# V weights early, K and Q weights as halves, remainder rows in one transfer, and a new written-out order

## The chip, the cores and the metric

One core of one Trainium2 chip. The metric is device time in microseconds (us) of one execution; the median of three runs of the kernel before is 170.06 us. PE is TensorE, DVE VectorE, ACT ScalarE, POOL GpSimd, and SP the engine whose queue issues nearly all transfers.

## The reference

A block with adaptive layer norm over x of 2048 x 448 (bfloat16): a sliding-window attention (16 heads of 28, each position sees 8 positions 2 apart) and a mixer MLP (448 to 1792 to 448).

```
mod = (silu(c) @ w_mod).reshape(...)           # sa, ca, ga, sb, cb, gb, 448 each
h = layernorm(x) * (1 + ca) + sa
q, k, v = split(h @ wqkv)                      # wqkv: 448 x 1344
o = softmax(q . k at 8 offsets, step 2) . v
x = x + ga * (o @ wo)
h = layernorm(x) * (1 + cb) + sb
x = x + gb * (gelu(layernorm(h) @ w1 + b1) @ w2 + b2)
```

## The kernel before

The 2048 rows are 8 tiles p of 2 x 128 rows. Per tile a layer norm (stats, rstd, normalize) gives zy, which is transposed and scaled by the modulation into hT (features on the partitions). Tiles 0 and 1 are transposed on PE (L534); tiles 2 to 7 by DMA transposes that SP issues (L526). Then K, Q and V projections, attention in 9 batches, output projection, second norms, and the MLP, whose two products (L547 with w1, L882 with w2) fill the second half of the run.

Inputs have 448 = 3 x 128 + 64 features. Each weight is therefore loaded as three full blocks of 128 rows and a **remainder** of 64 rows, which is stored twice, on partitions 0 to 63 and 64 to 127, so that two half-height matmuls can use both halves of the array. In the kernel before each copy of a remainder is a transfer of its own: two for the modulation (wm_r, L348), two for K and Q together (wqr_st, L328), two for V (Wv, L334). The three full blocks of K and Q come as one transfer per block, Q and K columns together (wqk_st, L324). "Spread" copies bring Q and K weights from wqk_st and wqr_st into Wqk and Wqr with 32 columns per head; they run on DVE, ACT or POOL (L438 to L449). For tiles 0 and 1 the projections of Q (half 0) and K (half 1) use Wqk and Wqr (`front_qk`, L561, L547, L553); tiles 2 to 7 use wqk_st and wqr_st directly (`natural_qk`).

Nothing is scheduled by the compiler. Every piece of work is recorded as a numbered task, and the string ORDER gives the sequence in which the tasks are written out: each engine executes its own tasks in just that sequence, and waits at the head of its queue for what its next task reads. `55+12@55` means that 12 dummy matmuls on a zero tile (`filler`, L381) are written ahead of task 55; a letter chooses the engine. SLOTS assigns each buffer its place in a pool. Transfers on SP go out in that order too, and eight completion counters take turns: a transfer is issued only after the one eight places ahead of it (ACT's two loads of c are counted in) has landed.

The loads stand in this order before the change: x tile 0, modulation weights (wm_st, then wm_r twice), x tile 1, K and Q weights block by block with their remainders between, x tiles 2 and 3, x tiles 6 and 7, V weights, x tiles 4 and 5. V of batches 0 and 1 is computed after K and Q of tiles 0 and 1.

Of the kernel before, what the change touches and what calls it, by code (L numbers as in the profile page):

```python
# [55 lines left out]
200 141 199 128 269 125 271 236 270 130 207 40 209 33 201 241 210 38 237 208 272 238 273 37 185 242 152 202 35 154 151
153:A 8 278 187 239 203 159 211 204 188 205:D 212 206 155 279 213 186 243 240 214:A 160 156 192 215 307 157 189 275
161 274 158 280 171 308 281 282 193 162 172 244 245 284 195 283 163 217 173 285 246 276:D 219 39 218 167 216 277 247
447 164 196 248 225 286 168 224 165 169:D 174 312 42 309 313 228 166 310 314 220 170 226 311 290 221 289 229 222 288
315 194 287 230 558 232 197 317 176 560 233 318 175 316 177 223 249 319 234 49 227 320 250 231 251 559 321 235 345 253  # L60
# [13 lines left out]
662 653 627 665 655 657 652 663 659 674 660 666 667 669 661 675 668 676 678 677 679 686 672 673 670 687 681 671 690
680 691 688 689 694 693 701 683 692 682 684 695 685 702 697 703 704 709 698 696 710 699 705 711 700 706 712 707 708
# [77 lines left out]
def kernel(  # L153
# [166 lines left out]
    def rows128(src):  # L320
        return src.rearrange("(k p) n -> p k n", p=128)

    def load_qk(kt):
        load(lambda: nc.sync.dma_start(out=wqk_st.t[:, kt, :], in_=A_wqkv[kt * 128:kt * 128 + 128, 0:2 * D + HP - DH]), 0.62, [f"wqk{kt}"],  # L324
             bufs=[wqk_st])

    def load_rest(a):
        load(lambda a=a: nc.sync.dma_start(out=wqr_st.t[KS * a:KS * a + KS, :], in_=A_wqkv[(KT - 1) * 128:D, 0:2 * D + HP - DH]),  # L328
             0.5, [f"wr{a}"], bufs=[wqr_st])
# [17 lines left out]
    for v in range(2):  # L347
        load(lambda v=v: nc.sync.dma_start(out=wm_r.t[KS * v:KS * v + KS, :], in_=w_mod[(KT - 1) * 128:D, v * D:v * D + D]),  # L348
             0.25, [f"wmr{v}"], bufs=[wm_r])
    for kt in range(KT - 1):  # L350
        load_qk(kt)
# [38 lines left out]
    add("PE", 0.45, c_cols, mode="32x128", reads=["c", "c1", "one1", "warm_w"], bufs=[psc], fills=[psc], name="c_cols")  # L390
    add("ACT", 0.12, lambda: nc.scalar.activation(out=e_c[:], in_=psc.t[:, 0, 0:128 * KT:128], func=ACT.Exp, scale=-1.0), bufs=[psc],
# [39 lines left out]
    def spread(half):  # L431
        def heads(ap, h):
            return bass.AP(ap.tensor, ap.offset, [*ap.ap[:-1], [DH, h], [1, HP]])

        for ks in [[k] for k in range(KT - 1)]:
            k0, n = ks[0], len(ks)
            dst, src = (lambda k0=k0, n=n: Wqk[:, k0:k0 + n, half]), (lambda k0=k0, n=n: heads(wqk_st.t[:, k0:k0 + n, half * D:half * D + D], H))
            add("DVE", 0.06 + 0.18 * n, lambda dst=dst, src=src: nc.vector.tensor_copy(out=dst(), in_=src()), reads=[f"wqk{k}" for k in ks],  # L438
                bufs=[wqk_st], writes=[f"W{half}{k}" for k in ks], port=True, name="spread",
                alt={"ACT": (0.13 + 0.43 * n, lambda dst=dst, src=src: nc.scalar.copy(out=dst(), in_=src())),  # L440
                     "POOL": (0.1 + 0.5 * n, lambda dst=dst, src=src: nc.gpsimd.tensor_copy(out=dst(), in_=src()))})

        for a in range(2):
            rows, c0 = slice(KS * a, KS * a + KS), half * D + a * D // 2
            src = lambda rows=rows, c0=c0: heads(wqr_st.t[rows, c0:c0 + D // 2], H // 2)
            add("DVE", 0.22, lambda rows=rows, src=src: nc.vector.tensor_copy(out=Wqr[rows, half], in_=src()), reads=[f"wr{a}"],
                bufs=[wqr_st], writes=[f"Wr{half}{a}"], port=True, name="spread r",
                alt={"ACT": (0.33, lambda rows=rows, src=src: nc.scalar.copy(out=Wqr[rows, half], in_=src())),
                     "POOL": (0.4, lambda rows=rows, src=src: nc.gpsimd.tensor_copy(out=Wqr[rows, half], in_=src()))})  # L449
# [59 lines left out]
    def front_ln(u, on_act, dma=False):  # L509
# [5 lines left out]
        for q, p in enumerate(u):  # L515
# [3 lines left out]
            rstd(0, 2 * p, 2, on_act)  # L519
# [59 lines left out]
    def front_qk(u):  # L579
        last_qk.clear()  # L580
        n, c0 = 128 * len(u), LEAD + 128 * u[0]
        for half in range(2):
# [30 lines left out]
    def natural_qk(p):  # L613
        c0 = LEAD + 128 * p
        for half in (1, 0):
# [6 lines left out]
            summed([item(s) for s in range(NS)], 0.1895, [f"wqk{k}" for k in range(KT - 1)] + ["wr0", "wr1"] + [f"h{kt}_{p}" for kt in range(KT)],  # L622
# [54 lines left out]
    def attention(i, tbl, prev_w1):  # L677
# [5 lines left out]
        if i not in DIRECT:  # L683
            hw = sb("hw", [128, KT, NS, 2, WK], BF16, "hw")

            def windows(copy):
# [8 lines left out]
                     lambda kt, rows: Wv[rows, kt, :]) for s in range(NS)], 0.1895, ["wv", "wvr0", "wvr1"],  # L695
                   [pv, vb, hw], [pv], f"v{i}")
        else:
# [19 lines left out]
            add("PE", 7 * 0.1895 + 0.1, None, reads=["pads", "wv", "wvr0", "wvr1"] + [f"h{kt}_{p}" for kt in range(KT) for p in ps_], bufs=[pv, vb],  # L717
# [244 lines left out]
```

## Time and profile before

| What | Value |
|---|---|
| median of 3 runs | 170.06 us (169.41 to 172.02) |
| the profiled execution | 170.37 us, of which 168.6 us lie between first and last instruction (the span) |
| PE busy | 160.9 us of the span |
| DVE, ACT, POOL busy | 113.2, 101.3, 42.0 us |
| moved by DMA | 18.78 MB, mean 111 GB/s |
| TensorE clock granted | 1.000 |

Times in the rows are us from the start of the span. A row of the timeline gives start, length, engine, source line, operation and tiles, a count, and in brackets how long the engine was idle before it and what ended that. The rows for stretches give, for each engine, busy us and (count).

### The profile page before, as it was taken

Reading aid. Unit: us, or ns where it says so; the run is one execution under the profiler, and the core shown is the slowest. Engines: PE = TensorE matmul, PEld = TensorE weight load, DVE = VectorE, ACT = ScalarE, POOL = GpSimd, SP = SyncE. Lnnn points to the kernel's source line nnn. Section 1 sums busy time; section 2 is a strip of 40 time slices with the busy share of each in tenths; the row PEclk is TensorE's granted clock in tenths of the full one; section 3 lists DMA queues with packets and bytes.
Section 4 is the critical chain, followed back from the end, with each engine's and each line's share of the span. In section 5 each row is a group of like instructions: output and inputs, shape, how many; then the busy total and the mean of one; then the engine's idle time right before and its main releaser. Section 6 shows DMA issues by size and latency. Waiting matters only on the chain.

```text
span 168.6 us, 4965 instructions
## 1 busy us (share of the span) xinstructions
PE 160.9 (95%) x2126; PEld 84.0 (50%) x2126; DVE 113.2 (67%) x277; ACT 101.3 (60%) x139; POOL 42.0 (25%) x69
## 2 busy tenths in 40 slices
PE   7999969987999999999999999999999999999992
PEld 4778535444554544435565443555544455344562
DVE  7869898758899969897837869465596940400112
ACT  3378888949379946869557167986318440099000
POOL 3235251002030400319300033850003156008100
PEclk9999999999999999999999999999999999999999
DMA  5999989699999799300150000028020006110002
GB/s 158 323 336 291 167 253 172 129 158 255 188 227 287 211 160 201 100 0 0 25 106 2 4 0 2 4 49 188 4 95 14 0 4 120 46 67 0 0 27 82
DMA packets 35573, 18.78 MB, mean 111 GB/s; under 512 B 28507, under 2 KB 34592, under 8 KB 35552
## 3 DMA queue, kind: packets, MB, share of 16 engines
q1 hardware_dynamic: 35548, 18.47, 47.6%
q8 instruction: 16, 0.26, 0.6%
q14 instruction: 5, 0.04, 0.1%
q10 hardware_dynamic: 4, 0.00, 0.0%
HBM read 9.81 MB, written 1.84 MB: 69 GB/s over the span
## 4 chain that ended last, share of the span: by engine, by line
PE 77%; DMA 13%; DVE 4%; issue 2%; POOL 2%; SPq 1%; ACT 1%; POOLq 0%; DVEq 0%
PE p L882 26%; PE p L547 22%; PE pw L802 7%; DMA zT<-zy 7%; PE pq L547 5%; PE p L553 4%; DMA x_all<-in_A_x_dram 4%; PE pv L547 3%; PE po L770 3%; DMA wm_st<-in_w_mod_dram 3%; PE lt L737 2%; DVE hT L501 2%; PE pv L705 2%; PE pd L759 1%; DVE stt L455 1%
## 5 line engine op out<-in xcount | busy, mean ns | idle before, releaser
L863 ACT ACTIVATE hm<-p,b_col 128x512 bf16<-128x512 f32 x56 | 33.6, 695 | 30.6 <-PE p L553 26.1
L882 PE MATMUL p<-w_s,hm 128*128 128x448 bf16 (+1 forms) x238 | 44.5, 342 | 0.0
L547 PE MATMUL p<-yT,w_s 128*128 128x512 bf16 x168 | 38.1, 380 | 0.0
L468 POOL TENSOR_TENSOR rs_all<-mvs,neg_half 128x2 f32<-128x2 f32 x23 | 16.4, 719 | 75.1 <-DVE mvs L457 75.1
L882 PEld LDWEIGHTS <-hm 128*128 128x128 bf16 x238 | 22.6, 98 | 18.9 <-issue 0.6
L547 PEld LDWEIGHTS <-w_s 128*128 128x128 bf16 x168 | 15.8, 98 | 21.0 <-issue 3.2
L888 DVE TENSOR_TENSOR x_all<-p,x1p 128x896 bf16<-128x896 f32 (+2 forms) x10 | 8.8, 899 | 23.7 <-PE p L882 23.7
L744 ACT ACTIVATE et<-lt 128x928 bf16<-128x928 f32 x18 | 16.1, 940 | 6.7 <-PE lt L737 6.6
L455 DVE BATCH_NORM_STATS2 stt<-x_all 128x6 f32<-128x448 bf16 x32 | 18.6, 610 | 1.6 <-DMA x_all<-in_A_x_dram 1.4
L547 PE MATMUL pq<-wqk_st,hT 128*128 128x448 bf16 x72 | 15.0, 353 | 1.8 <-DVE hT L501 1.5
L840 POOL TENSOR_TENSOR x1p<-x_all,gbb_bc 128x448 f32<-128x448 bf16 x16 | 16.5, 1060 | 0.0
L787 DVE TENSOR_TENSOR qT<-po,den 128x912 bf16<-128x912 f32 x9 | 10.0, 1106 | 7.1 <-ACT den L781 6.7
L802 PE MATMUL pw<-wo_s,qT 128*128 128x448 bf16 x64 | 13.1, 353 | 0.0
L750 DVE TENSOR_TENSOR et<-et,mask 128x928 bf16<-128x928 bf16 x18 | 11.0, 640 | 2.2 <-ACT et L744 2.1
L627 ACT CAST zy<-pq 128x896 bf16<-128x896 f32 x11 | 9.7, 911 | 2.7 <-issue 2.0
L809 DVE TENSOR_TENSOR x_all<-pw,x_all 128x896 bf16<-128x896 f32 x8 | 8.7, 1088 | 3.9 <-PE pw L802 3.9
L779 ACT ACTIVATE den<-pd 128x928 f32<-128x928 f32 x9 | 8.5, 952 | 4.7 <-PE pd L759 4.7
L818 DVE TENSOR_TENSOR h<-h,mod_bc 128x896 bf16<-128x896 bf16 x16 | 10.4, 655 | 0.2
L547 PEld LDWEIGHTS <-hT 128*128 128x128 bf16 x72 | 6.5, 98 | 8.1 <-DVE hT L501 2.0
L455 DVE BATCH_NORM_STATS2 stt<-h 128x6 f32<-128x448 bf16 x16 | 9.5, 611 | 0.1
L781 ACT ACTIVATE den<-den,den_bias 128x928 f32<-128x928 f32 x9 | 9.4, 1068 | 0.2
L802 PEld LDWEIGHTS <-qT 128*128 128x128 bf16 x64 | 6.0, 98 | 6.0 <-issue 0.4
(114 smaller groups left out, 177.3 us busy)
## 6 DMA issues: line engine op xcount, KB each, us to landing
w_s<-in_B_w_dram SPq DMA_DIRECT2D x7, 224.0 KB, 3.3
out_dram<-x_all SPq DMA_DIRECT2D x7, 224.0 KB, 2.0
x_all<-in_A_x_dram SPq DMA_DIRECT2D x3, 448.0 KB, 6.5
wmod<-in_w_mod_dram SPq DMA_DIRECT2D x3, 448.0 KB
w_s<-in_B_w_dram SPq DMA_DIRECT2D x3, 448.0 KB, 4.8
wqk_st<-in_A_wqkv_dram SPq DMA_DIRECT2D x3, 225.0 KB, 4.3
wm_st<-in_w_mod_dram SPq DMA_DIRECT2D x1, 672.0 KB, 4.6
x_all<-in_A_x_dram SPq DMA_DIRECT2D x2, 224.0 KB
```

The source lines that it names most:

```text
L455: add("DVE", 0.53, lambda: nc.vector.bn_stats(out=stt[:, w, b, 0:6], in_=src()), reads=reads, bufs=bufs, after=early if w == b == 0 else ( ...
L468: ways = {"POOL": (0.55 + 0.17 * n, lambda: nc.gpsimd.tensor_tensor(out=r, in0=v, in1=neg_half[:, 0:n], op=ALU.pow))}
L547: nc.tensor.matmul(out(), lhsT=lhs(kt, slice(0, 128)), rhs=rhs(kt, slice(0, 128)), start=first and kt == 0, stop=not first and kt == KT - 2)
L627: add("ACT", 0.80, lambda to=to, src=src: nc.scalar.copy(out=to(), in_=src()), bufs=[pq, st], reads=["zpad"], writes=[(st, 0)], name="evac ...
L744: exps.append(add("ACT", 0.83, lambda half=half, lt=lt: nc.scalar.activation(out=et.t[:, 2 * half:2 * half + 2].rearrange("p r m c -> p r ...
L750: nc.vector.tensor_tensor(out=ev, in0=ev, in1=mask[:], op=ALU.mult)
L787: nc.vector.tensor_tensor(out=qT[:, :, LEAD + q00:LEAD + q00 + 2 * WQ], in0=po.t[:, :, 0:NS * 4 * WQ].rearrange("p j (m c) -> p m j c", c=WQ),
L802: nc.tensor.matmul(pw.t[:, s, 0:D], lhsT=qT[:, KT * s + ft, LEAD + 128 * p:LEAD + 128 * p + 128], rhs=wo_s[:, ft, :], start=(ft == 0), sto ...
L818: add("DVE", 0.55, lambda vec=vec, op=op: nc.vector.tensor_tensor(out=h2.t[:], in0=h2.t[:], in1=vec.unsqueeze(1).to_broadcast([128, NS, D] ...
L840: add("POOL", 1.0, lambda n=n: nc.gpsimd.tensor_tensor(out=x1p.t[:, n, :], in0=xn(p, n), in1=gbb2_bc[:], op=ALU.add), reads=[f"x{p}", "gbb ...
L863: gelus.append(add("ACT", 0.585, lambda f=f, a=a, p1=p1s[g]: nc.scalar.activation(out=hm.t[:, f].rearrange("p n c -> p (n c)"), in_=p1.t[: ...
L882: nc.tensor.matmul(p2.t[:, n, 0:c1 - c0], lhsT=hm.t[:, f, n, q * 128:(q + 1) * 128], rhs=w2_s[:, f, c0:c1], start=(f == parts[0][0]), stop ...
```

## The change

1. Each remainder becomes one transfer (`twin`): the source is described as 2 x 64 rows, where the step of the outermost dimension is 448 columns for the modulation's and 0 for the others (the same 64 rows twice); the destination is 128 partitions. There are four: wm_r, Wv's, and one each for the K and the Q remainder.
2. The full blocks of K and Q come as two transfers, first all of K, later all of Q, instead of three transfers of both.
3. The V weights are loaded directly behind the modulation's; x tile 1, K and Q follow.
4. V of batch 0 stands in ORDER ahead of all K and Q projections. The layer norm of tile 0 takes its rstd one half at a time.
5. Dummy matmuls can be placed on carrier tasks of their own; 10 stand ahead of V of batch 0, 9 at the very end, 25 earlier (35 in all before the change, 44 after it). ORDER and SLOTS are new.

```diff
-    def load_qk(kt):
-        load(... out=wqk_st.t[:, kt, :], in_=A_wqkv[kt * 128:kt * 128 + 128, 0:2 * D + HP - DH]), 0.62, [f"wqk{kt}"], ...
-    def load_rest(a):
-        load(... out=wqr_st.t[KS * a:KS * a + KS, :], in_=A_wqkv[(KT - 1) * 128:D, 0:2 * D + HP - DH]), 0.5, [f"wr{a}"], ...
+    def load_half(half):
+        c0, c1 = half * D, half * D + D + half * (HP - DH)
+        load(... out=wqk_st.t[:, :, c0:c1], in_=rows128(A_wqkv[0:(KT - 1) * 128, c0:c1])), 1.15, [f"wqk{half}"], ...
+        load(... out=wqr_st.t[:, c0:c1], in_=twin(A_wqkv, c0, c1 - c0)), 0.4, [f"wr{half}"], ...
+
+    def twin(w, c0, n, step=0):
+        ld = w.ap[0][0]
+        return bass.AP(w.tensor, w.offset + (KT - 1) * 128 * ld + c0, [[step, 2], [ld, KS], [1, n]])
...
-        for a in range(2):
-            load(... out=Wv[KS * a:KS * a + KS, KT - 1, :], in_=A_wqkv[(KT - 1) * 128:D, 2 * D:3 * D]), 0.2, [f"wvr{a}"])
+        load(... out=Wv[:, KT - 1, :], in_=twin(A_wqkv, 2 * D, D)), 0.4, ["wvr"])
...
-    for v in range(2):
-        load(... out=wm_r.t[KS * v:KS * v + KS, :], in_=w_mod[(KT - 1) * 128:D, v * D:v * D + D]), 0.25, [f"wmr{v}"], ...
+    load(... out=wm_r.t[:], in_=twin(w_mod, 0, D, D)), 0.4, ["wmr"], bufs=[wm_r])
...
-            rstd(0, 2 * p, 2, on_act)
+            for b, m in ((2 * p, 1), (2 * p + 1, 1)) if p == 0 else ((2 * p, 2),):
+                rstd(0, b, m, on_act)
...
-3 14 17 0 1 15 5 9 10 18 11 16 13 19 20 2 6 24 21 73 55+12@55 26 12 71 25 56 72 74 57 75 22 58 77 23 59 62 60 27 61 76
+3 15 17 0 1 14 11 6 10 18 60+1@60 5 16 13 19 7 20 9 24 8 21 78 52+9@52 22 2 12 61 79 76 27 62 77 23 63 64 4 65 26 81
```

What stands in a row on the engines, at three places (names are tiles, destination before source; a count follows where rows are alike):

SP's queue at the program's start, before:

```order
L338 DMA x_all<-in_A_x_dram 128x896
L345 DMA wm_st<-in_w_mod_dram 128x3x896
L348 DMA wm_r<-in_w_mod_dram 64x448 x2
L338 DMA x_all<-in_A_x_dram 128x896
L324 DMA wqk_st<-in_A_wqkv_dram 128x900
L328 DMA wqr_st<-in_A_wqkv_dram 64x900 x2
L324 DMA wqk_st<-in_A_wqkv_dram 128x900 x2
L338 DMA x_all<-in_A_x_dram 128x2x896 x2
L332 DMA Wv<-in_A_wqkv_dram 128x3x448
```

SP's queue at the program's start, after:

```order
L338 DMA x_all<-in_A_x_dram 128x896
L345 DMA wm_st<-in_w_mod_dram 128x3x896
L347 DMA wm_r<-in_w_mod_dram 128x1x448
L334 DMA Wv<-in_A_wqkv_dram 128x3x448
L338 DMA x_all<-in_A_x_dram 128x896
L335 DMA Wv<-in_A_wqkv_dram 128x1x448
L326 DMA wqk_st<-in_A_wqkv_dram 128x3x452
L338 DMA x_all<-in_A_x_dram 128x2x896
L327 DMA wqr_st<-in_A_wqkv_dram 128x1x452
L327 DMA wqr_st<-in_A_wqkv_dram 128x1x448
L326 DMA wqk_st<-in_A_wqkv_dram 128x3x448
L338 DMA x_all<-in_A_x_dram 128x2x896 x2
```

V's weights moved from the thirteenth transfer to the fourth. The last Q weights went out as the tenth transfer; now they are the eleventh, behind all four remainders, whose rows read 128x1. L326 and L327 are `load_half`, L334 and L335 `load_wv`.

DVE's queue around the second norm of x tile 1 (zy) and the spreads (Wqk), before:

```order
L438 COPY Wqk<-wqk_st 128x512
L477 TENSOR_SCALAR zy_96<-x_all,mvs,rs_all 128x448 x2
L438 COPY Wqk<-wqk_st 128x512
L490 COPY zy_96<-zy_96 128x2x64
L438 COPY Wqk<-wqk_st 128x512
L455 BN_STATS stt<-x_all 128x6 x3
```

The same place on DVE, after:

```order
L438 COPY Wqk<-wqk_st 128x512
L477 TENSOR_SCALAR zy_96<-x_all,mvs,rs_all 128x448 x2
L455 BN_STATS stt<-x_all 128x6 x3
L457 BN_AGGR mvs<-stt 128x2 x2
L438 COPY Wqk<-wqk_st 128x512 x2
L455 BN_STATS stt<-x_all 128x6
L457 BN_AGGR mvs<-stt 128x2
L477 TENSOR_SCALAR zy_96<-x_all,mvs,rs_all 128x448 x2
```

Two spreads of the Q weights now stand between the statistics of x tiles 2 and 3 and the norms of those tiles; in the kernel before all spreads stood ahead of these statistics.

POOL's queue around its spreads (Wqk, Wqr), before:

```order
L300 MEMSET zy_100 128x32x4
L441 COPY Wqk<-wqk_st 128x512
L449 COPY Wqr<-wqr_st 64x256
L468 TENSOR_TENSOR rs_all<-mvs,neg_half 128x2
L449 COPY Wqr<-wqr_st 64x256
L468 TENSOR_TENSOR rs_all<-mvs,neg_half 128x2 x2
```

The same place on POOL, after:

```order
L289 COPY mask<-mask_90 128x928
L441 COPY Wqk<-wqk_st 128x512
L489 COPY zy_96<-zy_96 128x2x64
L449 COPY Wqr<-wqr_st 64x256 x4
L468 TENSOR_TENSOR rs_all<-mvs,neg_half 128x2
```

All four remainder spreads, two of K and two of Q, are now POOL's and stand in a row ahead of the rstd (rs_all) of x tile 3.

More of the change, by code (lines that the diff above doesn't have):

```diff
@@ L56 @@
[L56 to L60, printed above, removed]
@@ L74 @@
[L74 to L75 removed]
+3 15 17 0 1 14 11 6 10 18 60+1@60 5 16 13 19 7 20 9 24 8 21 78 52+9@52 22 2 12 61 79 76 27 62 77 23 63 64 4 65 26 81
+80 25 67 71 66 28 72 82 83 29 68+15@68 84 35 69 73 70 74 31 85 75 116 86 89 117 88 87 114 95:P 54+10@54 191:R 115 96
+118 97:A 119 120 107 148 192 108 121 109 99:P 150 122 98:P 141 93:P 110 124:A 112 94:P 111 149 91:A 151 90 152 92 139
@@ new lines @@
+100 126:A 101 102 125:A 142 153 103 105 113 154 104 140 123 155 204 156 132 143:A 106 145 127 144 206 146 196 147 286
+193 197 128 284 133 130 135 129 215 194 33 275 134 30 131 287 216 207 32 213 242 37 136 205 285 214 157 217 160 158:A
+159 244 208 247 245 161 288 209 210 277 211:A 243 165 212 218 219 248 195 220 166 246 221 162 170 167 198 169 249 163
+36 278 168 177 171 290 276 279 250 178 223 200 164 224 252 199 225 251 280 201 179 313 34 222:A 172 202 174 314:D 173
+253 180 203 238 175 254 318 53 239 289 319 227 315 226 316 320 291:D 281 240 292 230 317 282:D 228:D 283 321 322 323
@@ L76 @@
+593 590 656 622 640 621 591 623 639 594 624 657 670 595 652 596 625 597 649 598 627 651 664 628 626 629 660 630 668
+631 632:A 658 650 633 662 659 556 661 671 663 665 669 680 672 666 667 681 673 675 685 445 674 682 683 684 692 678 679
+693 687 694 686 676 677 696 699 698 703 691 697 695 690 700 707 688 689 701 702 704 708 711 709 705 59 712 710 715 713
+706 716 714 717 718 58+9@58
 """
@@ L321, in rows128 @@
         return src.rearrange("(k p) n -> p k n", p=128)
-    def load_qk(kt):
-        load(lambda: nc.sync.dma_start(out=wqk_st.t[:, kt, :], in_=A_wqkv[kt * 128:kt * 128 + 128, 0:2 * D + HP - DH]), 0.62, [f"wqk{kt}"],
-             bufs=[wqk_st])
-    def load_rest(a):
-        load(lambda a=a: nc.sync.dma_start(out=wqr_st.t[KS * a:KS * a + KS, :], in_=A_wqkv[(KT - 1) * 128:D, 0:2 * D + HP - DH]),
-             0.5, [f"wr{a}"], bufs=[wqr_st])
+    def load_half(half):
+        c0, c1 = half * D, half * D + D + half * (HP - DH)
+        load(lambda: nc.sync.dma_start(out=wqk_st.t[:, :, c0:c1], in_=rows128(A_wqkv[0:(KT - 1) * 128, c0:c1])), 1.15, [f"wqk{half}"], bufs=[wqk_st])
+        load(lambda: nc.sync.dma_start(out=wqr_st.t[:, c0:c1], in_=twin(A_wqkv, c0, c1 - c0)), 0.4, [f"wr{half}"], bufs=[wqr_st])
+    def twin(w, c0, n, step=0):
+        ld = w.ap[0][0]
+        return bass.AP(w.tensor, w.offset + (KT - 1) * 128 * ld + c0, [[step, 2], [ld, KS], [1, n]])
     def load_wv():
         load(lambda: nc.sync.dma_start(out=Wv[:, 0:KT - 1, :], in_=rows128(A_wqkv[0:(KT - 1) * 128, 2 * D:3 * D])), 1.15, ["wv"])
-        for a in range(2):
-            load(lambda a=a: nc.sync.dma_start(out=Wv[KS * a:KS * a + KS, KT - 1, :], in_=A_wqkv[(KT - 1) * 128:D, 2 * D:3 * D]),
-                 0.2, [f"wvr{a}"])
+        load(lambda: nc.sync.dma_start(out=Wv[:, KT - 1, :], in_=twin(A_wqkv, 2 * D, D)), 0.4, ["wvr"])
     def load_x(p0, p1):
@@ L346 @@
          2.1, ["wm0"], bufs=[wm_st])
-    for v in range(2):
[L348 to L351, printed above, removed]
+    load(lambda: nc.sync.dma_start(out=wm_r.t[:], in_=twin(w_mod, 0, D, D)), 0.4, ["wmr"], bufs=[wm_r])
+    load_wv()
+    load_half(1)
     load_x(1, 2)
-    load_rest(0)
-    load_rest(1)
+    load_half(0)
     load_x(2, 4)
-    load_wv()
     load_x(4, 6)
@@ L390 @@
     add("PE", 0.45, c_cols, mode="32x128", reads=["c", "c1", "one1", "warm_w"], bufs=[psc], fills=[psc], name="c_cols")
+    for i in range(8):
+        idle = psum("idle")
+        add("PE", 0.0, lambda: None, reads=["warm_w"], bufs=[idle], fills=[idle], instr=0, name=f"fl{i}")
     add("ACT", 0.12, lambda: nc.scalar.activation(out=e_c[:], in_=psc.t[:, 0, 0:128 * KT:128], func=ACT.Exp, scale=-1.0), bufs=[psc],
@@ L413, in modulation @@
         for i in range(2):
-            keys, st = (["wm0"], ["wmr0", "wmr1"])[i], (wm_st, wm_r)[i]
+            keys, st = (["wm0"], ["wmr"])[i], (wm_st, wm_r)[i]
             for a in range(2):
@@ L437, in spread @@
             dst, src = (lambda k0=k0, n=n: Wqk[:, k0:k0 + n, half]), (lambda k0=k0, n=n: heads(wqk_st.t[:, k0:k0 + n, half * D:half * D + D], H))
-            add("DVE", 0.06 + 0.18 * n, lambda dst=dst, src=src: nc.vector.tensor_copy(out=dst(), in_=src()), reads=[f"wqk{k}" for k in ks],
+            add("DVE", 0.06 + 0.18 * n, lambda dst=dst, src=src: nc.vector.tensor_copy(out=dst(), in_=src()), reads=["wqk1"] + ["wqk0"] * (1 - half),
                 bufs=[wqk_st], writes=[f"W{half}{k}" for k in ks], port=True, name="spread",
@@ L445, in spread @@
             src = lambda rows=rows, c0=c0: heads(wqr_st.t[rows, c0:c0 + D // 2], H // 2)
-            add("DVE", 0.22, lambda rows=rows, src=src: nc.vector.tensor_copy(out=Wqr[rows, half], in_=src()), reads=[f"wr{a}"],
+            add("DVE", 0.22, lambda rows=rows, src=src: nc.vector.tensor_copy(out=Wqr[rows, half], in_=src()), reads=[f"wr{half}"] + ["wr1"] * (1 - half) * a,
                 bufs=[wqr_st], writes=[f"Wr{half}{a}"], port=True, name="spread r",
@@ L598, in front_qk @@
                 last_qk.extend(summed([item(k, a) for a in range(2)], NS * n / 2400 + 0.0025,
-                                      ([] if first else [f"W{half}{k}" for k in range(KT - 1)] + [f"h{kt}_{p}" for kt in range(KT - 1) for p in u] + rk), [pqs[k]], [pqs[k]], after=last_qk[-2:] if small and k else (),
+                                      ([] if first else [f"W{half}{k}" for k in range(KT - 1)] + [f"h{kt}_{p}" for kt in range(KT - 1) for p in u] + rk), [pqs[k]], [pqs[k]], after=last_qk[-1 if u[0] == 0 else -2:] if small and k else (),
                                       name=f"qk{u[0]}_{half}" + "ab"[k], split=rk if first else None))
@@ L620, in item @@
                         lambda kt, rows: (wqk_st.t[:, kt] if kt < KT - 1 else wqr_st.t[rows])[:, half * D:half * D + D])
-            summed([item(s) for s in range(NS)], 0.1895, [f"wqk{k}" for k in range(KT - 1)] + ["wr0", "wr1"] + [f"h{kt}_{p}" for kt in range(KT)],
+            summed([item(s) for s in range(NS)], 0.1895, [f"wqk{half}", f"wr{half}"] + [f"h{kt}_{p}" for kt in range(KT)],
                    [pq, wqk_st, wqr_st], [pq], f"qk{p}_{half}n")
@@ L694, in attention @@
             summed([(lambda s=s: pv.t[:, s, 0:D], lambda kt, rows, s=s: hw.t[rows, kt, s].rearrange("p j c -> p (j c)"),
-                     lambda kt, rows: Wv[rows, kt, :]) for s in range(NS)], 0.1895, ["wv", "wvr0", "wvr1"],
+                     lambda kt, rows: Wv[rows, kt, :]) for s in range(NS)], 0.1895, ["wv", "wvr"],
                    [pv, vb, hw], [pv], f"v{i}")
@@ L715, in v_first @@
                 vmm(range(KT - 1), False)
-            add("PE", 7 * 0.1895 + 0.1, None, reads=["pads", "wv", "wvr0", "wvr1"] + [f"h{kt}_{p}" for kt in range(KT) for p in ps_], bufs=[pv, vb],
+            add("PE", 7 * 0.1895 + 0.1, None, reads=["pads", "wv", "wvr"] + [f"h{kt}_{p}" for kt in range(KT) for p in ps_], bufs=[pv, vb],
                 fills=[pv], instr=32, name=f"v{i}",
```

23 lines of the change are left out of this document (10 added, 13 removed), and 18 rows, old and new, of tables (ORDER, SLOTS).

## The prediction

> **What bounds the kernel now.** First the page's head, the division of the chain that ended last, and PE's busy time in stretches.
>
> ```profile
> span 168.6 us, 4965 instructions
> PE 160.9 (95%) x2126; PEld 84.0 (50%) x2126; DVE 113.2 (67%) x277; ACT 101.3 (60%) x139; POOL 42.0 (25%) x69
> PE 77%; DMA 13%; DVE 4%; issue 2%; POOL 2%; SPq 1%; ACT 1%; POOLq 0%; DVEq 0%
> ...
> 0.00:4.00 4.00, 2.75 (x13) 1.72 (x14) 2.81 (x20) 1.28 (x1) 1.43 (x11) 1.00 0.50 144
> 4.00:8.00 4.00, 4.00 (x55) 3.04 (x56) 3.53 (x20) 1.41 (x5) 0.51 (x1) 1.00 1.05 334
> ...
> 20.00:24.00 4.00, 2.53 (x52) 1.26 (x49) 3.32 (x11) 3.63 (x5) 2.94 (x4) 1.00 0.92 211
> ...
> 32.00:40.00 8.00, 6.24 (x164) 3.33 (x160) 5.85 (x12) 5.38 (x7) 0.17 (x1) 1.00 0.97 193
> 40.00:100.00 60.00, 60.00 (x914) 29.45 (x910) 49.70 (x102) 39.96 (x51) 12.60 (x17) 1.00 0.53 113
> 100.00:160.00 60.00, 60.00 (x568) 28.63 (x567) 29.70 (x63) 33.20 (x49) 18.96 (x24) 1.00 0.17 42
> 160.00:168.60 8.60, 5.64 (x44) 4.01 (x42) 1.78 (x3) 0.00 (x0) 0.00 (x0) 1.00 0.16 53
> ```
>
> From 40 to 160 us PE is busy all the time (60.00 of 60.00, twice), and the change removes no real matmul. So a microsecond counts only where it moves the moment at which PE has its steady supply. That is settled before 40 us, where PE stands idle 1.47 us (4.00 less 2.53) and 1.76 us (8.00 less 6.24), and where the chain consists of transfers:
>
> ```profile
> 1.26 4.57 DMA wm_st<-in_w_mod_dram
> ...
> 6.33 6.03 DMA x_all<-in_A_x_dram
> ...
> 17.61 3.41 DMA zT<-zy
> ...
> 21.12 1.81 DVE hT L501 x3
> 22.93 0.05 issue
> 22.97 2.44 PE pq L547 x12
> ```
>
> The modulation's weights land at 1.26 + 4.57 = 5.83 us, x tiles 2 and 3 at 12.36, and the first projection of tile 2 starts at **22.97 us**. I use that start as the mark: in both orders the same work precedes it (modulation, tiles 0 and 1, V, logits of batches 0 and 1), so its shift is the shift of PE's steady part.
>
> **The change part by part.** *Work moved on PE.* What PE does up to the mark:
>
> ```profile
> 1.25 2.74 PE L381 MATMUL ps_c<-warm_w 128*128 128x256 bf16 x12 [1.25 <-DVE warm_w L241]
> 8.26 1.14 PE L381 MATMUL pq<-warm_w 128*128 128x256 bf16 x9
> 9.78 1.31 PE L561 MATMUL pq<-hT,Wqk 128*128 128x256 bf16 x8
> 13.39 1.02 ACT L608 CAST qT<-pq 128x1024 bf16<-128x1024 f32 x1
> 14.29 1.04 ACT L608 CAST kT<-pq 128x1024 bf16<-128x1024 f32 x1
> 17.29 1.64 PE L705 MATMUL pv<-Wv,hT 128*64 128x448 bf16 x16
> 18.86 0.70 PE L737 MATMUL lt<-qT,kT 28*64 28x58 bf16 x64
> 19.79 0.95 ACT L744 ACTIVATE et<-lt 128x928 bf16<-128x928 f32 x1
> ```
>
> V of a batch costs 1.64. Today it runs behind K and Q; put first, it would fill time that dummy matmuls fill (8.26 to 9.40). That is a gain of up to 1.64 at the mark if the weights arrive as they do today. The 9 dummies at the program's end cost nothing: they take 1.14 and stand behind PE's last real matmul, and between that one and the end of the span are 2.96 us (8.60 less 5.64) of addition and stores. Splitting tile 0's rstd adds two ACT operations of 0.2, ahead of transfers that are later; nothing.
>
> *Transfers merged.* Two issues become one, four times over:
>
> ```profile
> 1.73 1.20 SPq L348 DMA_DIRECT2D wm_r<-in_w_mod_dram x2
> 4.08 1.11 SPq L328 DMA_DIRECT2D wqr_st<-in_A_wqkv_dram x2
> 7.46 0.62 ACT L440 COPY Wqk<-wqk_st 128x512 bf16<-128x512 bf16 x1 [1.00 <-DMA wqk_st<-in_A_wqkv_dram]
> 8.17 0.40 POOL L449 COPY Wqr<-wqr_st 64x256 bf16<-64x256 bf16 x1
> 10.67 0.28 DVE L438 COPY Wqk<-wqk_st 128x512 bf16<-128x512 bf16 x1
> ```
>
> An issue is some 0.6 (1.20 for two), so V and x tile 1 go out about 0.6 earlier. SP isn't what ends last there, so I count nothing. The open price is the **transfer itself**. Its source now has an outermost dimension of 2. How many of the 16 DMA engines share such a transfer? No row has one; bounds come from these:
>
> ```profile
> DMA packets 35573, 18.78 MB, mean 111 GB/s; under 512 B 28507, under 2 KB 34592, under 8 KB 35552
> q1 hardware_dynamic: 35548, 18.47, 47.6%
> q10 hardware_dynamic: 4, 0.00, 0.0%
> ...
> wo_s<-in_A_wo_dram SPq DMA_DIRECT2D x4, 98.0 KB
> ...
> yT<-zy SPq DMA_TRANSPOSE x8, 3.8
> zT<-zy SPq DMA_TRANSPOSE x6, 3.8
> kT<-zy SPq DMA_TRANSPOSE x6, 4.5
> qT<-zy SPq DMA_TRANSPOSE x6, 3.6
> ```
>
> Queue q10 holds the two one-row loads of c and shows 4 packets: one of data each, and one more. I read the extra as the completion mark of the one engine that each used. On q1 the same reading can be tested. Of the 28,507 packets under 512 B, 26,624 are the 26 transposes (1,024 pieces of 256 B for a 128 x 1024 tile), 256 the rows of the last two stores, 14 the bias rows, 3 belong to q10; 1,610 are left. If a transfer has one mark per engine, the 44 transfers of 128 or 64 rows on 16 engines make 704, the four wo_s of 28 rows on 14 engines 56, the bias (14 rows) 14, the four-row mod_hbm 4: 778, and the 832 left are exactly 32 for each transpose. With 16 for those of few rows nothing comes out even. So the number of engines follows the count of the outermost dimension. In those transfers source and destination have the same count. Here it is 128 against 2, and a source of 2 can be cut evenly only in two.
>
> The ends: on 16 engines a remainder of 114.7 kB (64 rows, twice, of 896 B) takes 114.7 / 334 = 0.34 us at the rate of the stretch 4 to 8; on two, at 334 / 16 = 20.9 kB per us each, 57.3 / 20.9 = **2.74 us**, and everything queued behind it on those two engines waits. I take two engines, since the count of packets follows the outermost dimension. [...]
>
> K and Q in rows of 904 and 896 B instead of 1,800 B I price at the same rate, as V's rows of 896 B go inside the same stretches.
>
> *What lands when, with two engines.* Each of the two carries, behind wm_st (5.83), in kB: wm_r 57.3, V 21.5, x tile 1 14.3, V remainder 57.3, K 21.7, x tiles 2 and 3 28.7, K remainder 57.9, Q remainder 57.3, Q 21.5. At 20.9 per us: wm_r 8.6; V remainder 13.0; K 14.1; K remainder 18.2; Q remainder 21.0; **Q 22.0**; the last x tiles 24.8. Today the last spread of a full block begins at 10.67.
>
> *What follows from 22.0.*
>
> ```profile
> 5.12 0.20 ACT L465 ACTIVATE rs_all<-mvs 128x2 f32<-128x2 f32 x1 [0.38 <-DVE e_c L393]
> ...
> 9.85 0.56 ACT L503 ACTIVATE hT<-ptr,mod_col 128x256 bf16<-128x256 bf16 x1
> ```
>
> Q's spreads stand in ACT's and DVE's rows: ACT 0.62, DVE twice 0.28. So DVE, with the norms of tiles 2 and 3 queued behind, stops too, and POOL's four remainder spreads hold back tile 3's rstd until 21.0 + 0.8. Tile 0's Q products run on PE beside ACT's work. On ACT stand, after the spread: two scalings of hT (0.56 each), K's evacuation 1.04, an rstd 0.4 (two of 0.20): 22.0 + 0.6 + 1.1 + 1.0 + 0.4 = 25.1, where Q's evacuation begins (13.39 today). Then Q 1.02, two exponentials 0.95 each, tile 1's Q and K 1.02 and 1.04, and logits on PE 0.70: 25.1 + 5.7 = 30.8, with a few semaphore gaps **31.0**. V of batch 1 (1.64) and tile 1's products fit beside that. The mark moves by 31.0 - 22.97 = +8.0.
>
> DVE's path to the mark agrees: its Q spreads end at 22.6, norms of tiles 2 and 3 stand behind statistics of x tile 4 (landing at 23.4) and end near 25.5, and the transposes take 3.41: 29, before 31.0. Behind the mark the statistics of the last tiles are, measured from the mark, earlier than today, so I let all of the 1.76 idle of 32 to 40 go. From 40 us on the new order can win nothing, PE being full, and can lose by gaps; PE has none today and I put none in. **Sum:** +8.0 - 1.8 = +6.2 against the profiled execution's 170.37 (span 168.6 and 1.8 around it) = 176.6; that execution lies 0.3 above the median, so I say **176.5**.
>
> Bounds: x tiles 2 and 3 have 107.8 kB per engine behind wm_st today, 5.2 us at that rate, and took 12.36 - 5.83 = 6.5, a factor of 1.26. The two engines are alone for much of the time, so I keep the full rate; with the factor Q lands 4.2 later (180.8). If the two engines finish wm_st 1 us before the slowest one does, and 1 us more is won behind the mark, it is 174.5.
>
> **The rivals.** *Sixteen engines after all (not slower).* The merged transfers cost 0.34 each. Behind wm_st stand 2,183 kB up to Q, 6.5 us at 334 GB/s, 8.2 with the factor 1.26: Q lands at 14.0, its evacuation begins 3.1 later, the mark comes at 17.1 + 5.9 = 23.0, as today. V is early but Q late. With the 1.76 idle kept 170.4, without it 168.6: **169.5**. For it: a descriptor list could be cut by rows whatever the dimensions; against it: the counts above. It decides at the point where the V remainder lands (about 8 or 13 us).
>
> [...]
>
> **How the numbers follow.** Forecast 0.62 (176.5, own range 174 to 178.5); slow PE 0.15 (177 to 180.5); sixteen engines 0.20 (167 to 172); 0.03 for a faster middle of another kind. About 2% is what a measurement can tell from no change: 173.5 and 166.7. Slower by over 2% 0.75, within 2% 0.20, faster 0.05. The range 169.5 to 180 leaves out half of the sixteen-engine case and little of the slow one.
>
> **What would show it.** Packets on q1: the K and Q blocks and remainders add 512 of data (384 + 128), and seven transfers of 16 marks fewer and four merged ones leave 35,956 with two engines and 36,012 with sixteen. The SP rows of wm_r should land 6 to 7 us after their issue, PE should stand idle for 5 us or more between 11 and 22, the waits should name wqk_st and wqr_st for 5 us on DVE and POOL, and the first L548 on tile 2 should start near 31 us. From 45 us on PE should be full as today; a gap there over 1 us would be a mistake of mine about the new order. If q1 shows 36,012, the forecast is wrong at its root.

## The result, and the profile after

The changed kernel takes **185.95 us** (median of 4, 184.62 to 186.9) against 170.38 for the kernel before: a ratio of 1.093, 95% interval 1.082 to 1.103. The profiled execution took 186.43 us.

The page's head, the count of q1 and the division of the chain, then busy time in stretches (PE, PEld, DVE, ACT, POOL; at the end PE's granted clock, the DMA share, GB/s):

```profile
span 184.3 us, 5003 instructions
q1 hardware_dynamic: 35956, 18.47, 45.7%
PE 73%; DMA 14%; SPq 6%; ACT 3%; DVE 1%; issue 1%; POOL 1%; DVEq 0%; ACTq 0%; POOLq 0%
12.00:16.00 4.00, 2.92 (x24) 1.44 (x22) 0.98 (x3) 2.09 (x5) 0.00 (x0) 0.89 0.17 59
16.00:20.00 4.00, 0.00 (x0) 0.00 (x0) 0.00 (x0) 0.10 (x1) 0.00 (x0) 0.96 0.90 271
20.00:24.00 4.00, 0.41 (x3) 0.28 (x4) 1.23 (x4) 0.00 (x0) 0.73 (x1) 0.50 0.77 208
24.00:32.00 8.00, 8.00 (x129) 5.83 (x128) 7.47 (x21) 5.35 (x10) 3.17 (x8) 0.84 0.26 54
40.00:60.00 20.00, 18.25 (x373) 9.00 (x372) 12.81 (x26) 13.86 (x17) 1.95 (x4) 0.91 0.92 145
100.00:160.00 60.00, 60.00 (x702) 29.36 (x701) 42.49 (x79) 32.67 (x45) 15.58 (x20) 1.00 0.21 39
```

35,956 packets is the two-engine count to the packet. Between 12 and 24 us PE works 3.3 of 12 us; 6% of the chain is now SP's queue, which had 1%. Next rows of SP's timeline, then of those of DVE, PE and ACT, and last a piece of the chain:

```profile
4.30 3.90 SPq L326 DMA_DIRECT2D wqk_st<-in_A_wqkv_dram  x1
9.16 3.51 SPq L327 DMA_DIRECT2D wqr_st<-in_A_wqkv_dram  x2
12.72 2.90 SPq L326 DMA_DIRECT2D wqk_st<-in_A_wqkv_dram  x1
...
9.38 0.18 DVE L417 COPY wm_d<-wm_r 128x64 bf16<-128x64 bf16 x1 [2.14 <-DMA wm_r<-in_w_mod_dram]
13.52 1.64 PE L706 MATMUL pv<-Wv,hT 64*64 64x448 bf16 x16 [0.23 <-DMA Wv<-in_A_wqkv_dram]
14.38 0.62 ACT L440 COPY Wqk<-wqk_st 128x512 bf16<-128x512 bf16 x1 [0.89 <-DMA wqk_st<-in_A_wqkv_dram]
22.77 0.29 DVE L438 COPY Wqk<-wqk_st 128x512 bf16<-128x512 bf16 x1 [9.75 <-DMA wqk_st<-in_A_wqkv_dram]
23.59 1.46 PE L562 MATMUL pq<-hT,Wqk 128*128 128x256 bf16 x6 [8.44 <-POOL Wqk L441]
25.94 0.56 ACT L503 ACTIVATE hT<-ptr,mod_col 128x256 bf16<-128x256 bf16 x1 [9.84 <-PE ptr L535]
26.41 0.61 ACT L440 COPY Wqk<-wqk_st 128x512 bf16<-128x512 bf16 x1
35.38 2.71 PE L548 MATMUL pq<-wqk_st,hT 128*128 128x448 bf16 x12 [0.27 <-DVE hT L501]
50.02 4.12 PE L548 MATMUL pq<-wqk_st,hT 128*128 128x448 bf16 x12
...
30.29 4.51 DMA zT<-zy
```

A row whose bracket names a DMA began when that transfer had landed: wm_r at 9.4, V's remainder 13.5, K 14.4. The mark comes at 35.38, 12.4 later than before. Behind it the span has 184.3 - 35.38 = 148.9 us left, 3.3 more than before (168.6 - 22.97 = 145.6). In what follows I split the span of each kernel's profiled execution in this way: the **mark**, and the **rest** of the span behind it.

Three rows were not foreseen. The copy at 22.77 is one of K's spreads, on DVE, 8 us after ACT's: DVE and POOL waited until Q had landed too. ACT's spread of Q stands behind a scaling that waits for tile 1's transposes on PE, and those stand behind tile 0's K products; it begins at 26.41. And the twelve matmuls at 50.02 take 4.12, where 2.44 was usual.

### The profile page after: what moved, and what is told of

It is laid out like the page before. It is cut to its first block, busy times and chain, and to the rows that moved or that the text cites. A ratio compares the mean times of both kernels' runs of the same rounds, so it can differ in the third digit from the quotient of the medians.

```text
span 184.3 us, 5003 instructions
## 1 busy us (share of the span) xinstructions
PE 167.0 (91%) x2135; PEld 86.4 (47%) x2135; DVE 117.8 (64%) x270; ACT 102.7 (56%) x145; POOL 46.9 (25%) x74
## 3 DMA queue, kind: packets, MB, share of 16 engines
q1 hardware_dynamic: 35956, 18.47, 45.7%
## 4 chain that ended last, share of the span: by engine, by line
PE 73%; DMA 14%; SPq 6%; ACT 3%; DVE 1%; issue 1%; POOL 1%; DVEq 0%; ACTq 0%; POOLq 0%
PE p L883 23%; PE p L548 20%; PE pw L803 7%; DMA zT<-zy 6%; PE pq L548 6%; DMA wqk_st<-in_A_wqkv_dram 5%; PE p L554 4%; PE pv L548 3%; PE lt L738 2%; DMA kT<-zy 2%; PE po L771 2%; SPq L326 2%; SPq L327 2%; PE pv L706 2%; ACT hT L503 1%
## 5 line engine op out<-in xcount | busy, mean ns | idle before, releaser
L864 ACT ACTIVATE hm<-p,b_col 128x512 bf16<-128x512 f32 x56 | 34.1, 689 | 26.7 <-PE p L554 23.1
L548 PE MATMUL pq<-wqk_st,hT 128*128 128x448 bf16 x72 | 16.9, 383 | 0.3 <-DVE hT L501 0.3
L841 POOL TENSOR_TENSOR x1p<-x_all,gbb_bc 128x448 f32<-128x448 bf16 x16 | 17.0, 1088 | 0.0
L819 DVE TENSOR_TENSOR h<-h,mod_bc 128x896 bf16<-128x896 bf16 x16 | 11.6, 726 | 0.3
L477 DVE TENSOR_SCALAR zy<-h,mvs,rs_all 128x448 bf16<-128x448 bf16 x16 | 8.6, 569 | 4.5 <-POOL rs_all L468 2.4
L503 ACT ACTIVATE hT<-ptr,mod_col 128x256 bf16<-128x256 bf16 x5 | 2.6, 562 | 14.6 <-PE ptr L535 14.6
L562 PE MATMUL pq<-hT,Wqk 128*128 128x256 bf16 x12 | 2.3, 343 | 8.4 <-POOL Wqk L441 8.4
```

Source lines behind the costliest of these rows:

```text
L548: nc.tensor.matmul(out(), lhsT=lhs(kt, slice(0, 128)), rhs=rhs(kt, slice(0, 128)), start=first and kt == 0, stop=not first and kt == KT - 2)
L819: add("DVE", 0.55, lambda vec=vec, op=op: nc.vector.tensor_tensor(out=h2.t[:], in0=h2.t[:], in1=vec.unsqueeze(1).to_broadcast([128, NS, D] ...
L841: add("POOL", 1.0, lambda n=n: nc.gpsimd.tensor_tensor(out=x1p.t[:, n, :], in0=xn(p, n), in1=gbb2_bc[:], op=ALU.add), reads=[f"x{p}", "gbb ...
L864: gelus.append(add("ACT", 0.585, lambda f=f, a=a, p1=p1s[g]: nc.scalar.activation(out=hm.t[:, f].rearrange("p n c -> p (n c)"), in_=p1.t[: ...
```

## The experiments

**1. Pairs again.** In the changed kernel, each merged remainder is two transfers of 64 rows (shown for K and Q; the other two are changed alike).

```diff
-    dma_start(out=wqr_st.t[:, c0:c1], in_=twin(A_wqkv, c0, c1 - c0))
+    for a in range(2):
+        dma_start(out=wqr_st.t[KS * a:KS * a + KS, c0:c1], in_=A_wqkv[(KT - 1) * 128:D, c0:c1])
```

> The new order and the halves stay; each merged remainder is two transfers of 64 rows again (8 in place of 4). Theory A (a transfer whose outermost count is 2 runs on two DMA engines, and that holds up SP, Q's landing and with it the mark): all four stalls go, Q lands near 14 us, the mark comes at 22 to 24 us, 169 to 172.5 us in all, 36,076 packets on q1 (120 more marks). Theory B (the new order and the halves are what costs): still over 180 us. If K's spreads, which wait for Q's block as well, cost much even then, something between, 173 to 177.

**2. Merging alone**, in the kernel before (its order and its blocks of K and Q).

> The kernel before, in its own order and with its own blocks of K and Q, but with its three pairs of remainders each merged into one transfer with outermost count 2. Theory A: on the two engines wm_r lands at 8.6, K and Q's remainder (115 kB each, 5.5 us) near 15.5, the last block of K and Q near 17 in place of 10; mark 5 to 8 us later, 175 to 180 us, 35,458 packets on q1. Theory B: as before, 169.5 to 171.5 us.

**3. Outermost count 2 without merging**, and **4. merging without it** (the latter leaves the two copies in neighbouring partitions).

```diff
-    [[step, 2], [ld, KS], [1, n]]     # the change: 128 rows as 2 x 64
+    [[ld, 2], [2 * ld, 32], [1, n]]   # 3: each 64 rows as 2 x 32
+    [[ld, KS], [step, 2], [1, n]]     # 4: 128 rows as 64 x 2
```

> As the first of these kernels (eight transfers of 64 rows, nothing merged), but each one's source is described with outermost count 2: the even rows, then the odd ones (so the remainder's weights stand in another order and those products sum other terms). Theory A, the outermost count decides: two engines for each, 35,964 packets on q1, as slow as the change, 183 to 188 us. Rival: it is the merge (one transfer to 128 partitions, or the repeated reading of the same rows) that confines it; then as the first kernel, 169 to 172.5 us and 36,076 packets.

> As the change, with its four merged transfers, but the source's two outer dimensions exchanged: 64 rows outside, the two copies inside (so the copies lie in neighbouring partitions, and the remainder's products take wrong rows). Same bytes, same number of issues, same destination. Theory A: sixteen engines, 36,012 packets on q1, 168.5 to 172.5 us. Rival (the merge itself is slow): as the change, 184 to 187 us.

| Kernel | q1 packets | mark | rest | ratio to before (95%) |
|---|---|---|---|---|
| before | 35,548 | 22.97 | 145.6 | 1 |
| the change | 35,956 | 35.38 | 148.9 | 1.093 (1.082 to 1.103) |
| 1 pairs | 36,076 | 27.45 | 147.5 | 1.037 (1.028 to 1.045) |
| 2 merging alone | 35,458 | 30.73 | 145.7 | 1.044 (1.035 to 1.052) |
| 3 count 2, pairs | 35,964 | 35.31 | 147.5 | 1.087 (1.079 to 1.095) |
| 4 count 64, merged | 36,012 | 24.54 | 150.7 | 1.042 (1.035 to 1.050) |

All four counts are as expected, kernels 2 (176.96 us) and 3 (184.47 us) came within the times expected of them, and the kernels fall in two groups by the outermost count, not by merging: 1 and 4 against 3 and the change. That is **shown**: the outermost count of the source decides, and it costs 8.2 to 9.7 us here (184.47 in 3 against 176.23 in 1, and 185.95 in the change against 177.01 in 4 and 176.23 in 1). SP's queue tells the same; the issues of K and Q blocks in kernel 2 (two of them), then in kernel 4 (one):

```profile
4.00 3.07 SPq L324 DMA_DIRECT2D wqk_st<-in_A_wqkv_dram  x2
...
4.21 0.59 SPq L326 DMA_DIRECT2D wqk_st<-in_A_wqkv_dram  x1
```

Kernel 2 also shows what the mark is worth: in the order of before its shift of 7.8 goes whole into the span of the profiled execution, and the rest stays at 145.7. Kernel 4 was to come at 168.5 to 172.5 and took 177.01. Kernel 1 missed the 169 to 172.5 of its theory, though 176.23 lies within the 173 to 177 that its text names for the case that the wait of K's spreads costs much. So some 6 to 7 us (against 169.82 for the kernel before in the same measurement) are the new order's and the halves'.

**5. K and Q in separate halves of the staging tile**, in the changed kernel, and **6. the same with pairs** (experiment 1). The remainders' tile wqr_st is divided in the same way.

```diff
-    wqk_st = sb("hm", [128, KT - 1, 2 * D + HP - DH], BF16, "wqk_st")
+    wqk_st = sb("hm", [128, 2, KT - 1, D + HP - DH], BF16, "wqk_st")
```

> As the change, merged transfers included, but the staging tile of K and Q holds K's columns and Q's columns in two separate halves, so that no address of K's lies between two of Q's. Theory C (K's spreads wait for Q's transfer only because the two lie interleaved in one tile): DVE's and POOL's K spreads begin near 14.5 us, as ACT's did, in place of 22.8; K's products run before Q lands at 22.7; the mark falls from 35.4 to 31 to 33 us and the time to 181 to 184 us. Rival: Q's landing sets the mark anyway, then the spreads begin early and the time stays at 185 to 187 us.

> The first experiment's kernel (remainders as pairs of 64 rows) with the separate halves besides. Theory C: no wait of K's spreads for Q; PE has no 3.7 us of idleness at 11 to 15 us, so it doesn't run slowly at 16 to 20 us either; mark at 22.5 to 25 us in place of 27.5, 172.5 to 175 us. If the rest of the loss lies behind the mark (the order of the norms and transposes of the last tiles, theory D), part of what the mark wins is given back there, and it stays near 175 to 176.5 us.

POOL's and PE's timelines in kernel 5, then PE's in kernel 1, then PE's in kernel 6 and two pieces of its chain:

```profile
13.14 0.74 POOL L441 COPY Wqk<-wqk_st 128x512 bf16<-128x512 bf16 x1 [8.73 <-DMA wqk_st<-in_A_wqkv_dram]
13.94 0.83 PE L562 MATMUL pq<-hT,Wqk 128*128 128x256 bf16 x6
...
14.78 1.46 PE L569 MATMUL pq<-hT,Wqk 128*128 128x256 bf16 x6 [3.66 <-POOL Wqk L448]
...
10.51 1.64 PE L713 MATMUL pv<-Wv,hT 64*64 64x448 bf16 x16
12.08 0.83 PE L569 MATMUL pq<-hT,Wqk 128*128 128x256 bf16 x6
23.14 2.71 PE L555 MATMUL pq<-wqk_st,hT 128*128 128x448 bf16 x12 [0.28 <-DVE hT L508]
...
10.61 6.18 DMA x_all<-in_A_x_dram
...
18.42 4.16 DMA zT<-zy
```

Kernel 5: K's products run at 13.94 in place of 23.59, mark 32.37, 183.8 us, ratio 1.080 (1.072 to 1.087). Kernel 6: mark 23.14, 173.67 us, 1.022 (1.016 to 1.029). Both came within what was expected. Theory C is **shown**: with the halves apart the wait is gone, and K's products run 9.65 us earlier. What that is worth in time is less sharp: the intervals of 5 and the change overlap, and those of 6 and 1 touch. Kernel 6 also gives back part of what it wins at the mark: its rest is 149.1, where kernel 1 had 147.5. In the interleaved tile blocks 0 and 1 of K lie between columns of Q: in each partition Q's write reaches from element 0 to 2248 of 2700, and K's first two blocks are 448 to 900 and 1348 to 1800. Only block 2 (2248 to 2700) lies outside, and its spread is the one that ran at 14.38.

**7. PE kept busy** in the changed kernel: `107` in ORDER becomes `107+66@107`.

> As the change, with 66 dummy matmuls of 128x256 (some 7.4 us) on PE between the first V products and K's first products, where PE stood idle from 15.2 to 23.6 us. Theory: the slow stretch behind the gap (granted clock 0.50 to 0.84 from 20 to 32 us) comes from the gap; with the dummies K's products and the next transposes run at 0.13 us each and the mark comes 1 to 2 us earlier, 184 to 185.5 us. Rival: ACT and DVE set the pace there and PE's speed doesn't count: 185.5 to 187 us.

181.97 us, ratio 1.072 (1.066 to 1.078): the largest gain of a single edit that keeps the two-engine transfers, but not at the place I named. It is faster than the 184 to 185.5 expected. The mark falls only to 34.65; the rest falls by 3.0, to 145.9. Stretches of this kernel, then the twelve matmuls that took 4.12 in the change, then stretches of kernel 11 (below), which is the change with one copy moved and no such dummies:

```profile
24.00:32.00 8.00, 7.52 (x133) 5.64 (x134) 7.95 (x22) 5.95 (x10) 3.17 (x8) 1.00 0.47 60
40.00:60.00 20.00, 18.61 (x446) 10.19 (x436) 15.52 (x30) 14.37 (x18) 3.08 (x4) 1.00 1.00 176
...
47.99 2.44 PE L548 MATMUL pq<-wqk_st,hT 128*128 128x448 bf16 x12
...
20.00:24.00 4.00, 1.83 (x12) 1.46 (x13) 2.65 (x6) 0.00 (x0) 1.95 (x5) 0.50 0.50 140
40.00:60.00 20.00, 18.82 (x455) 10.04 (x444) 16.15 (x33) 15.18 (x18) 2.79 (x4) 1.00 0.90 162
```

In kernel 7 the clock is 1.00 in both stretches, where the change has 0.84 and 0.91. That the gap of PE ahead of K's products lowers the clock behind it is shown. The slow row at 50 us is another matter: kernels 11 and 3 keep the gap, show a clock of 0.50 from 20 to 24 us like the change, and have 1.00 from 40 to 60. Why PE is slow again there in the change stays open.

**8. Norms of tiles 6 and 7 earlier on DVE** (in 6), **9. and the tail copy of tile 5 on DVE** ahead of the masks, **10. and two loads of w_s later**, **11. the tail copy alone** in the changed kernel.

```diff
-... 290 276 279 250 ... 280 201 ... 289 319 ... 291:D 281 ... 282:D
+... 290 289 291:D 276 279 250 ... 280 281 282:D 201 ...
-... 219 248 195 220 166 ...
+... 219 220:D 248 195 166 ...
```

(In the first of these texts "the second of these kernels" is kernel 6; in the third "the kernel before this one" is kernel 9.)

> As the second of these kernels, with one edit of the order table: on DVE the second norm and the tail of x tiles 6 and 7 stand right behind their first norms, no longer behind the masks, products and copies of batches 0 to 2. Theory D (what is left against before is the late third pair of transposes, 15.6 us behind the mark in place of 9.3, and the transposes of Q and K queued behind them on SP): that pair begins some 2 us earlier, the 2 us gap of PE before the logits of batch 4 shrinks, 1.5 to 3 us faster than the second of these kernels. Rival: the transposes are late for another reason (the queue of SP, or the buffers), no difference.

> As the kernel with the norms moved (pairs of 64 rows, separate halves, norms of tiles 6 and 7 earlier), with one more edit of the order: the tail copy of x tile 5 runs on DVE, ahead of the masks of batches 0 and 1, no longer on POOL. Theory E (POOL's copy took 2.23 us in place of 0.29 because DVE's masks ran beside it, and the second pair of zT and all of SP behind it waited for that): the second transpose of the pair starts near 25.5 in place of 27.3, tile 2's Q and K transposes some 1.5 us earlier, PE's gaps of 0.9 and 0.8 us between 29 and 37 shrink; 1 to 2 us faster, 170.5 to 172 us. Rival: the transposes' own transfers set the pace (the loads before them fill the queue); no difference, 172.5 us.

> As the kernel before this one in the list, with the two loads of w_s that stand on SP between the transposes of tiles 4 and 5 moved behind tile 5's. If the last gap (1.2 us before the logits of batch 4, near 50 us) comes from those loads, it shrinks and the time falls by 0.5 to 1 us more, 169.5 to 171.5 us, which is level with the kernel before the change or just under it. Rival: the gap has another cause and the time stays.

> As the change itself (merged transfers, interleaved halves), with the tail copy of x tile 5 on DVE ahead of the masks and nothing else. Theory E: 1 to 2 us faster than the change, 184 to 185 us, the second transpose of zT's second pair 2 us earlier behind the mark. Rival: hidden behind the other waits, 185.5 to 187 us.

POOL's and DVE's timelines in the change, SP's there, and SP's in kernel 11:

```profile
37.84 2.23 POOL L489 COPY zy<-zy 128x128 bf16<-128x128 bf16 x1 [2.16 <-issue]
37.63 2.29 DVE L751 TENSOR_TENSOR et<-et,mask 128x928 bf16<-128x928 bf16 x4
...
36.99 5.10 SPq L527 DMA_TRANSPOSE zT<-zy  x2
...
35.47 2.62 SPq L527 DMA_TRANSPOSE zT<-zy  x2
```

With the copy on DVE the pair of transposes is out after 2.62 instead of 5.10, in kernel 11 as in 9 (2.63). In kernel 3, where POOL's copy took 1.68, it was out after 2.64 as well.

How the rest divides is told by PE's busy time from the mark to 160 us, here for the kernel before, the change, 3, 7 and 11:

```profile
22.97:160.00 137.03, 135.26 (x1773) 65.93 (x1774) 92.57 (x196) 86.24 (x115) 33.20 (x43) 1.00 0.43 91
35.38:160.00 124.62, 121.99 (x1692) 59.24 (x1693) 95.20 (x189) 80.71 (x106) 33.67 (x41) 0.99 0.50 97
35.31:160.00 124.69, 121.25 (x1707) 59.57 (x1699) 94.83 (x186) 80.48 (x106) 32.90 (x40) 1.00 0.48 93
34.65:160.00 125.35, 123.93 (x1721) 60.43 (x1713) 97.61 (x190) 81.53 (x108) 34.27 (x41) 1.00 0.49 101
34.42:160.00 125.58, 122.53 (x1715) 59.94 (x1709) 95.85 (x187) 80.46 (x106) 31.12 (x40) 1.00 0.46 94
```

The first number less the second is what PE stands idle there; the table has it as gaps.

| Kernel | mark | rest | gaps | ratio to before (95%) |
|---|---|---|---|---|
| before | 22.97 | 145.6 | 1.77 | 1 |
| the change | 35.38 | 148.9 | 2.63 | 1.093 (1.082 to 1.103) |
| 3 count 2, pairs | 35.31 | 147.5 | 3.44 | 1.087 (1.079 to 1.095) |
| 7 dummies | 34.65 | 145.9 | 1.42 | 1.072 (1.066 to 1.078) |
| 11 tail alone | 34.42 | 147.3 | 3.05 | 1.081 (1.078 to 1.084) |
| 5 apart | 32.37 | 149.5 | 3.57 | 1.080 (1.072 to 1.087) |
| 6 apart, pairs | 23.14 | 149.1 | 4.54 | 1.022 (1.016 to 1.029) |
| 8 norms | 22.56 | 147.8 | 3.26 | 1.022 (1.013 to 1.031) |
| 9 and tail | 23.15 | 146.8 | 2.49 | 1.012 (1.008 to 1.016) |
| 10 and loads | 23.23 | 146.3 | 2.00 | 1.011 (1.007 to 1.016) |

The rest of 11 is 1.6 shorter than the change's, but not by its gaps, which are longer: what it lacks is the slow row at 50 us, and so does 3, which leaves the copy on POOL. So the 1.6 doesn't show what the copy is worth. From 6 over 8 and 9 to 10 the gaps and the rest fall step by step, one profiled execution each; the times hardly tell even 6 and 10 apart, and the intervals of 8 and 9, of 9 and 10, and of 11 and the change overlap. So theories D and E are not settled. Kernel 8 (172.70 us) moved the third pair from 15.6 to 14.7 us behind the mark and was to be 1.5 to 3 us faster than 6 (173.67); it is 1.0 faster, within the noise. 11 (183.72 us) came just under the 184 to 185 of its theory, but not by the gaps that the theory was about. 10 (172.17 us against 169.5 to 171.5) is level with 9. None is faster than before: the best, 10, is about 1% slower, with V first as in the change.

## Why the prediction was wrong

The direction was right, the size was not: forecast 176.5 us with a range to 180, measured 185.95. (The 0.3 that was taken off the sum of 176.6 would have given 176.3.) Of the 9.8 us between the sum and the profiled execution, 4.4 lie at the mark, 5.1 behind it and 0.4 around the span.

- **Two engines:** right. The count is exact, and the landings came at 9.4, 13.5 and 14.4 where 8.6, 13.0 and 14.1 were worked out; Q was due at 22.0 and DVE's spread started at 22.77. That the number of engines follows the outermost dimension fits the packet counts of all six kernels of the first table (35,956 in the change with 2 outside, 36,012 in kernel 4 with 64). Kernel 1, with two transfers for each remainder, is 9.7 us faster than the change.
- **"SP isn't what ends last there, so I count nothing":** wrong in the trace. An issue of K took 3.90 and a pair of remainders 3.51, so Q's went out only at 12.72 (6.86 in kernel 4). At Q's landing the forecast was off by 0.7 (22.7 against 22.0), so leaving it out cost little there.
- **"What follows from 22.0":** the first step that failed. I had K's spreads done from 14.1 on and tile 0's K products beside the wait for Q. DVE's and POOL's waited for Q as well, 9.75 us on DVE, because the transfers overlap in addresses of one tile: in kernel 5, with the halves apart, POOL's K spread began at 13.14 in place of 22.80. Then everything behind K's products was late: ACT's spread of Q, which I had at 22.0, began at 26.41, 4.4 late, as much as the mark. The chain runs from there over an rstd on ACT, tile 3's norm on DVE and transposes that end at 34.8; that is the path I had at 29, not the one over Q's evacuation. With the halves apart the mark came at 32.37, near my 31.0. PE started slowly behind its gap (0.24 a matmul at 23.59, against 0.14 in kernel 6). No run shows the loss behind the 177 to 180.5 that I gave 0.15 for a slow PE; in kernel 7, which fills the gap, the mark came 0.7 earlier.
- **"I let all of the 1.76 idle go", "I put none in":** the second step that failed, and the larger one. In place of -1.8 the part behind the mark gave +3.3. PE's gaps there did not go; they are 2.63, 0.9 more than before. And the sum had no term for slow matmuls behind the mark: the rows at 35.38 and 50.02 take 0.3 and 1.7 more than 2.44 each. Some 0.5 more is not placed. In kernel 7 both parts are smaller (gaps of 1.42, no such row at 50 us), and its rest is 145.9. What makes PE slow at 50 us, and which part of the new order makes the gaps, stays open.
- **The rival of sixteen engines (169.5):** would have been as wrong. Kernel 4 is that rival, and it took 177.0. I had its mark at 23.0 and behind it at most the gaps of before. It came at 24.5 with 5.0 more behind, where PE's gaps up to 160 us are 4.20 in place of 1.77 and the matmuls at 54 us are slow. Kernel 10, with pairs, is 4 us faster than 1 after the separate halves and the three moves in the order; about 2 us of it against before stay open.
- **V first:** no gain at the mark, as I had for the rival. In kernel 6 V runs at 10.5 in place of 17.3 us and the mark is 23.14 against 22.97: the bracket at 23.14 names hT. Its chain goes through a transfer of x that lands at 16.8 (10.61 + 6.18), behind V, K and Q on SP, and the transposes at 18.42; in the chain of before x landed at 12.36 and they stood at 17.61.

## What to carry to other kernels

Before merging transfers, count the outermost dimension of the source: with 2 x 64 rows it had the packet count of two engines here, Q's issue behind it came at 12.72 in place of 6.86, and the kernel took 8.9 us longer than with 64 x 2 (185.95 against 177.01). When one tile is filled by several transfers, see that no reader's columns lie between those of a later transfer: here the reader then waited for both, and with the halves apart K's products ran 9.65 us earlier. An order that was fitted to other durations need not keep PE full when these change: price gaps and slow matmuls behind the mark, not only what lies ahead of it. And before a gain is put down to an edit, see where in the trace it lies: the 1.6 us of kernel 11 lie in a row that the edit does not touch.

## What the hardware showed unexpectedly

SP's issue of a transfer itself took longer behind those with outermost count 2. K's issue took 3.90 us in the change and 0.59 in kernel 4, which differs in the outermost count alone; in kernel 3 it took 1.13. From 12 to 16 us, where Q's issue took 2.90, the change's DMA moved 59 GB/s.

POOL's copy of 128x128 values took 2.23 us beside DVE's masks (copy 37.84 to 40.07, masks 37.63 to 39.92), and 0.29 the three times before it in the change, where no mask ran (0.29 to 0.64 the four times later). In kernel 8 it took 2.23 beside them again (copy from 25.02, masks 24.81 to 27.10). No run moves the masks alone, so that they slow the copy is my reading of these rows.

The clock does not follow the length of the last gap alone. After 3.66 us idle K's products in kernel 1 took 0.24 us each (clock 0.68 from 12 to 16 us and 0.50 from 16 to 20); after 1.90 in kernel 4 they took 0.14 (1.00 in both). But with nearly the same gap further on, 2.07 and 2.08, twelve matmuls took 3.66 in kernel 4 and 2.44 in kernel 6 (clock from 40 to 60 us 0.91 and 1.00; the first three rows are kernel 4's):

```profile
13.34 0.83 PE L562 MATMUL pq<-hT,Wqk 128*128 128x256 bf16 x6 [1.90 <-POOL Wqk L441]
...
54.22 0.22 PE L738 MATMUL lt<-qT,kT 28*64 28x58 bf16 x3 [2.07 <-issue]
54.37 3.66 PE L548 MATMUL pq<-wqk_st,hT 128*128 128x448 bf16 x12
...
53.03 0.22 PE L745 MATMUL lt<-qT,kT 28*64 28x58 bf16 x3 [2.08 <-issue]
53.18 2.44 PE L555 MATMUL pq<-wqk_st,hT 128*128 128x448 bf16 x12
```
